# A decode block on one core: `w_out` in 96 partitions, the gated MLP in nine chunks of 96, and a query projection with one head to each group of 32 partitions

## The chip, the core and the metric

The kernel runs on one core of one Trainium2 chip. The metric is the device time of one execution in microseconds, the median of three runs. The core has a matrix engine (PE, with its weight loads listed as PEld), a vector engine (DVE), a scalar engine (ACT), GpSimd (POOL) and a sync engine (SP) that here does nothing but issue transfers. Transfers between HBM and the on-chip SBUF are carried by 16 DMA engines. Matmul results are written to PSUM.

## The reference, cut to what matters

Batch 4, one new token each, D = 640. Attention has 32 heads of 128 over a cache of 4096 positions; the gated MLP has 2 x 864 columns (F = 1728, Fh = 864). Everything is bf16 at the border.

```python
xn = _layernorm(x)
# attention: read the whole key and value cache
q = (xn @ wq).reshape(B, 1, 32, 128).transpose(0, 2, 1, 3)
p = softmax(einsum('bhqd,bhkd->bhqk', q, k_cache) * 128 ** -0.5)
A = (einsum('bhqk,bhkd->bhqd', p, v_cache)).transpose(...).reshape(B, 1, 4096) @ wo
# gated MLP
z = gelu(xn @ w_in)
z1, z2 = z[..., :864], layernorm(z[..., 864:])
g = w_sp * z2 + b_sp
Bm = (z1 * g) @ w_out
out = x + A + Bm
```

The two caches are 4 x 32 x 4096 x 128 bf16 each, 134 MB; the weights are small beside them (`wq` and `wo` 5.2 MB each, `w_in` 2.2 MB, `w_out` 1.1 MB).

## The kernel before, in words

**Tiles.** The cache is cut into 32 key tiles and 32 value tiles. Tile i holds four heads (head group i // 4) of one batch row (i % 4): 4 x 4096 positions, laid over 128 partitions, so that each head has 32 partitions and each partition 128 positions of 128 numbers, 32 KB that lie together in HBM. One tile is 4096 KB and one transfer.

**Slots and the order of transfers.** Five SBUF slots of tile size (`kv`, L69) rotate. The first three hold weights: `wq` in two pieces (L87 to L90) and `w_sb`, in which `w_in` and `w_out` lie side by side (L97 to L104). `w_out` has 864 rows of 1280 bytes. Before, its first 768 rows go to 128 partitions, six rows each (L101), and the other 96 rows to 96 partitions, one row each (L104). Then SP issues key tiles 0 and 1 and from there on, by the list of L125 to L132, a value tile and a key tile in turn. `pump()` (L137) issues the next one as soon as the program has passed the work on the tile that had the slot; on the chip the issue waits for that work through semaphores. `wo` comes in eight pieces of 640 KB (L147), the last one in four.

**Before the loop.** `xn` is normalised and transposed to `xnT` (128 partitions x 5 chunks x 32 columns, of which 4 are used). The query projection (L211 to L226) runs in two rounds r. In a round the four head groups g of that round each write 32 partitions of one PSUM tile: 5 chunks x 4 groups = 20 matmuls of 512 columns, and one DVE copy makes `q_rows[r]`. A row of `q_rows[r]` is then one head group and batch row, its 512 columns the four heads of that group.

**`stage_q(i)`** (L379) spreads the query of tile i over all partitions: a matmul with a repeated column of the identity as weights copies one row of `q_rows` to 128 partitions (512 columns, L384), and four ACT copies of 32 partitions each take the right head's 128 columns (L394).

**`gmlp()`** (L268) computes the gated MLP transposed: for each half t of `w_in` and each of seven chunks of its columns (six of 128, one of 96), five matmuls give `zT` (L276, 70 in all). DVE copies `zT` in two pieces (L283, L284) into `zz`, which POOL has cleared (L262), and computes the gelu with one ACT tanh. The sums of z2 and of its square are 14 matmuls of four columns with a column of ones (L302). After the layernorm and the gate, 14 matmuls with `w_out` add to `out_ps` (L366).

**The loop** over the 32 key tiles (L568) is in an order written by hand (`manual_schedule`, for PE, DVE, ACT and SP). For tile i in two halves: DVE multiplies the half with the query in place (`product`, L400), adds the two halves of the head dimension (`fold_half`, L409), PE adds up to eight numbers (`sums`, L418) and DVE the rest (`row_sums`, L429). `head_max` (L436) finds the maximum over each head's 32 partitions, negated, `exps` (L445) scales it on ACT to `nb` (L448) and makes the exponentials with their sums, a head at a time (L453). `weighted` (L462) multiplies them with the value tile on PE. `stage_q(i + 2)` stands in the middle of iteration i. Once in four tiles `group_den`, `group_pick`, `group_turn` and `group_proj` (L484 to L536) finish a head group and add its product with `wo` to `out_ps`.

**The end.** Value tile 31 comes in four pieces (L113), and its 128 matmuls (L625) have the value tile as weights. Then `o_n_last` (L633), eight matmuls with the last `wo` (L530), two copies and two transfers out (L640 to L643).

**Waits of SP.** Each transfer waits, besides for its slot, for the landing of the transfer eight before it in the program, whose semaphore it takes over (the first eight are free of that; three of the eight are small ones that ACT issues at L83, L94 and L95).

Of the kernel before, what the change touches and what calls it, by code (L numbers as in the profile page):

```python
# [9 lines left out]
FP32 = mybir.dt.float32  # L10
BF16 = mybir.dt.bfloat16
ACT = mybir.ActivationFunctionType
ALU = mybir.AluOpType
AX = mybir.AxisListType
# [7 lines left out]
def kernel(  # L22
# [14 lines left out]
    nc = tc.nc  # L37
    P = nc.NUM_PARTITIONS
    Bsz, Sq, D = A_x.shape
    _, H, S, Dh = A_k_cache.shape  # L40
    HD = A_wq.shape[1]
    F = B_w_in.shape[1]
    Fh = F // 2
    DC = D // P
    scale_qk = float(Dh) ** -0.5
# [3 lines left out]
    HT = 4  # L49
    HG = H // HT  # L50
    NT = HG * Bsz
    LN = P // HT
# [2 lines left out]
    HD2 = Dh // 2  # L55
    RW = 8
    SLOT = NC * Dh
    NFF = Fh // P
    NFC = NFF + 1
    FT = Fh - NFF * P  # L60
    NOH = D // 2
    QD = 32
    CB = 4
    NG = NC // CB
    GW = CB * Dh
    MC = CB * HT

    const = ctx.enter_context(tc.tile_pool(name="const", bufs=1))
    kv = ctx.enter_context(tc.tile_pool(name="kv", bufs=KV_SLOTS))  # L69
    wop = ctx.enter_context(tc.tile_pool(name="wop", bufs=WO_BUFS))  # L70
    work = ctx.enter_context(tc.tile_pool(name="work", bufs=1))
    small = ctx.enter_context(tc.tile_pool(name="small", bufs=2))
    PSUM = bass.MemoryType.PSUM
    ps_s = ctx.enter_context(tc.tile_pool(name="ps_s", bufs=2, space=PSUM))
    ps_pv = ctx.enter_context(tc.tile_pool(name="ps_pv", bufs=2, space=PSUM))
    ps_m = ctx.enter_context(tc.tile_pool(name="ps_m", bufs=3, space=PSUM))
# [9 lines left out]
    wq_parts = []  # L86
    for c0, c1 in ((0, HT), (HT, DC)):  # L87
        t = slot("wq")[:, 0 : (c1 - c0) * HD].rearrange("p (c n) -> p c n", n=HD)
# [9 lines left out]
    w_in_sb = w_sb[:, 0 : DC * F].rearrange("p (c n) -> p c n", c=DC)  # L98
    w_out_sb = w_sb[:, DC * F : DC * F + NFC * D].rearrange("p (k n) -> p k n", k=NFC)
    nc.sync.dma_start(out=w_in_sb, in_=B_w_in.rearrange("(p c) n -> p c n", c=DC))  # L100
    nc.sync.dma_start(  # L101
        out=w_out_sb[:, 0:NFF, :], in_=B_w_out[0 : NFF * P].rearrange("(p k) n -> p k n", k=NFF)
    )
    nc.sync.dma_start(out=w_out_sb[:FT, NFF, :], in_=B_w_out[NFF * P : Fh])  # L104

    def kv_view(cache, i):
        hg, b = divmod(i, Bsz)
# [51 lines left out]
    ident = const.tile([P, P], BF16)  # L159
# [2 lines left out]
    nc.vector.memset(ones_row[:], 1.0)  # L162
    eps_tile = const.tile([P, 1], FP32)
    nc.vector.memset(eps_tile[:], eps)
    ones_sq = const.tile([P, P], FP32)
    nc.vector.memset(ones_sq[:], 1.0)

    NACC = 2
    p_m = [const.tile([P, NG, QD], BF16, name=f"pm{b}") for b in range(Bsz)]
    acc = [const.tile([P, HT, QD], FP32, name=f"acc{g}") for g in range(NACC)]  # L170
# [9 lines left out]
    for i in range(NSTAT):  # L180
# [5 lines left out]
        out=rstd[:], in_=mv[:, 1:2], func=ACT.Sqrt, bias=eps_tile[:Bsz], scale=1.0  # L186
# [4 lines left out]
        out=xn_bf[:],  # L191
        in0=x_bf[:],
        scalar1=mv[:, 0:1],
        scalar2=rstd[:],
        op0=ALU.subtract,
# [5 lines left out]
    for c in range(DC):  # L201
        nc.tensor.transpose(
            out=xnT_ps[:, c, :], in_=xn_v[:, c, :], identity=ident[:Bsz, :Bsz]
# [5 lines left out]
    QB = HG // CB  # L209
    q_rows = []  # L210
    for r in range(QB):  # L211
        q_ps = ps_pv.tile([P, GW], FP32, tag="pv", name="q_ps")
        for c in range(DC):
            t, i = wq_parts[c]
            for g in range(CB):
                hg = r * CB + g
                nc.tensor.matmul(  # L217
                    out=q_ps[g * QD : (g + 1) * QD, :],
                    lhsT=xnT[:, c, :],
                    rhs=t[:, i, hg * GW : (hg + 1) * GW],  # L220
                    start=(c == 0),
                    stop=(c == DC - 1),
                )
        rows = const.tile([P, GW], BF16, name=f"q_rows{r}")
        nc.vector.tensor_copy(out=rows[:], in_=q_ps[:])  # L225
        q_rows.append(rows)  # L226

    pick = const.tile([P, 2, CB, HT, QD], FP32)
# [3 lines left out]
        out=hot[:],  # L232
        in_=ident[:].rearrange("p (g t m) -> p t m g", g=P // QD, t=2),
        axis=AX.X,
        op=ALU.add,
    )
    for a in range(2):
        for t in range(2):
            nc.vector.tensor_copy(
                out=pick[:, a, :, :, 2 * a + t],  # L240
# [16 lines left out]
        )  # L257

    gm = {}
    for name in ("zz", "gw", "gt", "gz"):  # L260
        gm[name] = work.tile([P, 2, NFC, Bsz], FP32, name=name)
    nc.gpsimd.memset(gm["zz"][:], 0.0)  # L262
    gm["sq"] = work.tile([P, NFC, Bsz], FP32, name="sq")
    gm["st"] = work.tile([1, 5 * Bsz], FP32, name="st")
    gm["ac"] = work.tile([1, 2 * Bsz], FP32, name="ac")
    gm["yT"] = work.tile([P, NFC, Bsz], BF16, name="yT")

    def gmlp():  # L268
        zz, gw, gt, gz, sq = (gm[n] for n in ("zz", "gw", "gt", "gz", "sq"))
        zT = ps_pv.tile([P, 2, NFC, Bsz], FP32, tag="pv", name="zT")  # L270
        for t in range(2):
            f1 = t * Fh + NFF * P
            w_t = w_in_sb[:, :, t * Fh : f1].rearrange("p c (f k) -> p c k f", k=NFF)
            for k in range(NFC):
                for c in range(DC):
                    nc.tensor.matmul(  # L276
                        out=zT[: P if k < NFF else FT, t, k, :],
                        lhsT=w_t[:, c, k, :] if k < NFF else w_in_sb[:, c, f1 : f1 + FT],
                        rhs=xnT[:, c, 0:Bsz],
                        start=(c == 0),  # L280
                        stop=(c == DC - 1),
                    )
        nc.vector.tensor_copy(out=zz[:, :, 0:NFF, :], in_=zT[:, :, 0:NFF, :])  # L283
        nc.vector.tensor_copy(out=zz[:FT, :, NFF, :], in_=zT[:FT, :, NFF, :])  # L284
        nc.vector.tensor_tensor(out=gw[:], in0=zz[:], in1=zz[:], op=ALU.mult)
        nc.vector.tensor_scalar(
            out=gw[:], in0=gw[:], scalar1=0.044715, scalar2=1.0, op0=ALU.mult, op1=ALU.add
# [5 lines left out]
        nc.vector.tensor_scalar(  # L293
            out=gt[:], in0=gt[:], scalar1=1.0, scalar2=0.5, op0=ALU.add, op1=ALU.mult
        )
        nc.vector.tensor_tensor(out=gz[:], in0=zz[:], in1=gt[:], op=ALU.mult)
        nc.vector.tensor_tensor(out=sq[:], in0=gz[:, 1, :, :], in1=gz[:, 1, :, :], op=ALU.mult)

        s_ps = ps_m.tile([1, 2 * Bsz], FP32, tag="m", name="ln_ps")
        for src, at in ((gz[:, 1, :, :], 0), (sq[:], Bsz)):  # L300
            for k in range(NFC):
                nc.tensor.matmul(  # L302
                    out=s_ps[:, at : at + Bsz],
                    lhsT=ones_sq[:, 0:1],
                    rhs=src[:, k, :],
                    start=(k == 0),
                    stop=(k == NFC - 1),
                )
        st, ac = gm["st"], gm["ac"]
        mean_t = st[:, 0:Bsz]  # L310
        ex2_t = st[:, Bsz : 2 * Bsz]
        var_t = st[:, 2 * Bsz : 3 * Bsz]
        rst_t = st[:, 3 * Bsz : 4 * Bsz]
        tmp_t = st[:, 4 * Bsz : 5 * Bsz]
        nc.vector.tensor_scalar(
            out=st[:, 0 : 2 * Bsz],
            in0=s_ps[:],
            scalar1=1.0 / float(Fh),
            scalar2=None,
            op0=ALU.mult,  # L320
# [27 lines left out]
        ac_sb = work.tile([P, 2 * Bsz], FP32, name="ac_sb")  # L348
        nc.scalar.copy(out=ac_sb[:], in_=ac_ps[:])
        nc.vector.tensor_tensor(  # L350
            out=sq[:],
            in0=gz[:, 1, :, :],
            in1=ac_sb[:, None, 0:Bsz].to_broadcast([P, NFC, Bsz]),
            op=ALU.mult,
        )
        nc.vector.tensor_tensor(
            out=sq[:],
            in0=sq[:],
            in1=ac_sb[:, None, Bsz : 2 * Bsz].to_broadcast([P, NFC, Bsz]),
            op=ALU.add,  # L360
        )
        nc.vector.tensor_tensor(out=gm["yT"][:], in0=gz[:, 0, :, :], in1=sq[:], op=ALU.mult)
        for k in range(NFC):
            w = P if k < NFF else FT
            for half in range(2):
                nc.tensor.matmul(  # L366
                    out=out_sum(half),
                    lhsT=gm["yT"][:w, k, :],
                    rhs=w_out_sb[:w, k, half * NOH : (half + 1) * NOH],
                    start=False,  # L370
                    stop=False,
                )
# [6 lines left out]
    def stage_q(i):  # L379
        hg, b = divmod(i, Bsz)  # L380
        r, g = divmod(hg, CB)
        row = g * QD + b
        qb_ps = ps_m.tile([P, HT, Dh], FP32, tag="m", name="qbc_ps")
        nc.tensor.matmul(  # L384
            out=qb_ps[:],
            lhsT=ident[:, row : row + 1].to_broadcast([P, P]),
            rhs=q_rows[r][:],
            start=True,
            stop=True,
        )  # L390
        qbcs[i] = small.tile([P, Dh], BF16, name="qbc", bufs=3)
        for hh in range(HT):
            ps = slice(hh * LN, (hh + 1) * LN)
            nc.scalar.copy(out=qbcs[i][ps, :], in_=qb_ps[ps, hh, :])  # L394

    def half_of(i, half):
        return k_tiles[i][:, half * HC : (half + 1) * HC, :]
# [46 lines left out]

    def exps(i):  # L445
        hg, b = divmod(i, Bsz)
        nb = small.tile([P, 1], FP32, name="nb")
        nc.scalar.mul(out=nb[:], in_=maxes.pop(i)[:], mul=scale_qk)  # L448
        s_sb, a = scores.pop(i), acc[hg % NACC]
        pm = p_m[b][:].rearrange("p g (t c h) -> p g t c h", t=2, c=CB)  # L450
        for hh in range(HT):
            ps = slice(hh * LN, (hh + 1) * LN)
            nc.scalar.activation(  # L453
                out=pm[ps, :, b % 2, :, hh],
                in_=s_sb[ps, :].rearrange("p (g c) -> p g c", c=CB),
                func=ACT.Exp,
                bias=nb[ps],
                scale=scale_qk,
                accum_out=a[ps, hh, b : b + 1],
            )  # L460

# [212 lines left out]
```

## Time and profile before

| What | Before |
|---|---|
| Median of 3 runs (lowest, highest) | 666.81 us (666.65, 666.91) |
| The profiled execution's own time | 666.78 us |
| Its span, first to last instruction | 665.0 us |
| Busy: PE, DVE, ACT, POOL | 309.9, 499.5, 127.1, 4.7 us |
| Read from HBM | 282.24 MB |
| Rate over the span | 424 GB/s |
| Mean granted PE clock | 0.715 of full |

The span leaves out 1.78 us that belong to the execution's time. An engine's busy time says how long it had work, not that it set the end: DVE is the busiest and is idle a quarter of the time. The DMA rows count packets; a packet is one contiguous piece of a transfer, and each of the 16 engines also writes one 4-byte completion per transfer. The trace keeps a start, a duration and a size for each packet.

### The profile page before, as it was taken

Reading aid. Unit: us, or ns where it says so; the run is one execution under the profiler, and the core shown is the slowest. Engines: PE = TensorE matmul, PEld = TensorE weight load, DVE = VectorE, ACT = ScalarE, POOL = GpSimd, SP = SyncE. Lnnn points to the kernel's source line nnn. Section 1 sums busy time; section 2 is a strip of 40 time slices with the busy share of each in tenths; the row PEclk is TensorE's granted clock in tenths of the full one; section 3 lists DMA queues with packets and bytes.
Section 4 is the critical chain, followed back from the end, with each engine's and each line's share of the span. In section 5 each row is a group of like instructions: output and inputs, shape, how many; then the busy total and the mean of one; then the engine's idle time right before and its main releaser. Section 6 shows DMA issues by size and latency. Waiting matters only on the chain.

```text
span 665.0 us, 5142 instructions
## 1 busy us (share of the span) xinstructions
PE 309.9 (47%) x2033; PEld 130.3 (20%) x2033; DVE 499.5 (75%) x350; ACT 127.1 (19%) x441; POOL 4.7 (1%) x15
## 2 busy tenths in 40 slices
PE   2536443445436235553238443355443655338466
PEld 1312111211112111321113111131111312113124
DVE  2299797877788777788777697777787899776970
ACT  0302222102222111222111222111222122111121
POOL 2000000000000000000000000000000000000000
PEclk9656766877767777776776856788765678776575
DMA  9999999999999999999999999999999999999996
GB/s 367 430 440 417 434 436 426 433 430 429 436 420 440 426 430 437 426 431 428 432 433 424 435 434 424 438 421 440 427 430 436 423 436 426 433 432 430 431 430 274
DMA packets 11972, 282.58 MB, mean 425 GB/s; under 512 B 1344, under 2 KB 1964, under 8 KB 3244
## 3 DMA queue, kind: packets, MB, share of 16 engines
q1 hardware_dynamic: 11928, 282.25, 99.2%
q8 instruction: 16, 0.26, 0.2%
q14 instruction: 8, 0.07, 0.0%
q10 hardware_dynamic: 20, 0.01, 0.0%
HBM read 282.24 MB, written 0.01 MB: 424 GB/s over the span
## 4 chain that ended last, share of the span: by engine, by line
DMA 68%; DVE 23%; PE 6%; issue 2%; SPq 0%; DVEq 0%
DMA k_nat<-in_A_k_cache_dram 62%; DVE k_nat L400 12%; DVE k_nat L409 7%; PE s_ps L418 4%; DMA v_nat<-in_A_v_cache_dram 4%; DVE s_sb L429 2%; DMA wq<-in_A_wq_dram 2%; PE pv L470 1%; PE q_ps L217 1%; DVE m L438 0%; DVE mt L440 0%; DVE o_n L513 0%; DVE nm L442 0%; PE out_ps L530 0%; SPq L120 0%
## 5 line engine op out<-in xcount | busy, mean ns | idle before, releaser
L400 DVE TENSOR_TENSOR k_nat<-k_nat,qbc 128x8192 bf16<-128x8192 bf16 x64 | 282.7, 4417 | 104.6 <-DMA k_nat<-in_A_k_cache_dram 104.3
L418 PE MATMUL s_ps<-k_nat,ident 128*128 128x512 bf16 x512 | 183.8, 523 | 327.0 <-DVE k_nat L409 327.0
L418 PEld LDWEIGHTS <-ident 128*128 128x128 bf16 x512 | 62.3, 122 | 430.7 <-issue 356.8
L409 DVE TENSOR_TENSOR k_nat<-k_nat 128x4096 bf16<-128x4096 bf16 x64 | 146.0, 2281 | 0.0
L448 ACT ACTIVATE nb<-nm 128x1 f32<-128x1 f32 x32 | 6.5, 203 | 355.1 <-DVE nm L442 355.1
L470 PE MATMUL pv<-v_nat,pm 128*32 128x512 bf16 x992 | 71.0, 438 | 3.7 <-DMA v_nat<-in_A_v_cache_dram 3.7
L453 ACT ACTIVATE pm<-s_sb,nb 32x128 bf16<-32x128 f32 x128 | 71.7, 560 | 2.7
L394 ACT CAST qbc<-qbc_ps 32x128 bf16<-32x128 f32 x128 | 32.8, 256 | 133.1 <-PE qbc_ps L384 132.0
L429 DVE TENSOR_REDUCE s_sb<-s_ps 128x64 f32<-128x512 f32 x64 | 43.6, 682 | 3.1 <-PE s_ps L418 3.1
L470 PEld LDWEIGHTS <-pm 128*32 128x32 bf16 x992 | 25.9, 109 | 55.3 <-issue 36.9
L453 ACT ACTIVATION_READ_ACCUMULATOR pm<-s_sb,nb 32x1 f32 x128 | 30.1, 235 | 0.0
L502 PEld LDWEIGHTS o_ps<-o_rows,pick 128*128 128x128 f32 x112 | 20.1, 269 | 2.1 <-issue 1.4
L502 PE MATMUL o_ps<-o_rows,pick 128*128 128x128 f32 x112 | 19.5, 347 | 0.0
L384 PE MATMUL qbc_ps<-q_rows,ident 128*128 128x512 bf16 x32 | 17.5, 552 | 0.0
L482 ACT COPY o_rows<-pv 128x512 f32<-128x512 f32 x16 | 9.4, 585 | 27.5 <-PE pv L470 27.5
L494 DVE RECIPROCAL rden<-den 128x1 f32<-128x1 f32 x7 | 1.2, 168 | 15.6 <-PE den L486 15.6
L438 DVE TENSOR_REDUCE m<-s_sb 128x1 f32<-128x128 f32 x32 | 9.2, 286 | 1.1
L225 DVE CAST q_rows<-q_ps 128x512 bf16<-128x512 f32 x2 | 1.4, 692 | 10.6 <-PE q_ps L217 10.6
L440 DVE STREAM_TRANSPOSE mt<-m 128x32 f32<-128x32 f32 x32 | 6.8, 212 | 1.1
L217 PE MATMUL q_ps<-wq,xnT 128*32 128x512 bf16 x40 | 4.1, 552 | 7.3 <-DMA wq<-in_A_wq_dram 7.3
L442 DVE TENSOR_REDUCE nm<-mt 128x1 f32<-128x32 f32 x32 | 6.0, 186 | 1.1
L384 PEld LDWEIGHTS <-ident 128*128 128x128 bf16 x32 | 4.4, 141 | 8.6 <-issue 8.6
(83 smaller groups left out, 73.4 us busy)
## 6 DMA issues: line engine op xcount, KB each, us to landing
k_nat<-in_A_k_cache_dram SPq DMA_DIRECT2D x32, 4096.0 KB, 41.2
v_nat<-in_A_v_cache_dram SPq DMA_DIRECT2D x31, 4096.0 KB, 35.7
wo<-in_A_wo_dram SPq DMA_DIRECT2D x7, 640.0 KB, 42.3
wq<-in_A_wq_dram SPq DMA_DIRECT2D x1, 4096.0 KB, 12.8
w_sb<-in_B_w_in_dram SPq DMA_DIRECT2D x1, 2160.0 KB, 19.5
v_nat<-in_A_v_cache_dram SPq DMA_DIRECT2D x1, 2048.0 KB
wq<-in_A_wq_dram SPq DMA_DIRECT2D x1, 1024.0 KB, 14.8
v_nat<-in_A_v_cache_dram SPq DMA_DIRECT2D x1, 1024.0 KB
```

The source lines that it names most:

```text
L217: nc.tensor.matmul(out=q_ps[g * QD : (g + 1) * QD, :], lhsT=xnT[:, c, :], rhs=t[:, i, hg * GW : (hg + 1) * GW], start=(c == 0), stop=(c == ...
L384: nc.tensor.matmul(out=qb_ps[:], lhsT=ident[:, row : row + 1].to_broadcast([P, P]), rhs=q_rows[r][:], start=True, stop=True,)
L394: nc.scalar.copy(out=qbcs[i][ps, :], in_=qb_ps[ps, hh, :])
L400: nc.vector.tensor_tensor(out=half_of(i, half), in0=half_of(i, half), in1=qbcs[i][:, None, :].to_broadcast([P, HC, Dh]), op=ALU.mult,)
L409: nc.vector.tensor_tensor(out=t[:, :, 0:HD2], in0=t[:, :, 0:HD2], in1=t[:, :, HD2:Dh], op=ALU.add)
L418: nc.tensor.matmul(out=s[:], lhsT=ident[:], rhs=t[:, :, g * RW : (g + 1) * RW], start=(g == 0), stop=(g == n - 1),)
L429: nc.vector.tensor_reduce(out=scores[i][:, half * HC : (half + 1) * HC], in_=sums_ps.pop((i, half))[:], axis=AX.X, op=ALU.add,)
L438: nc.vector.tensor_reduce(out=m1[:], in_=scores[i][:], axis=AX.X, op=ALU.max)
L453: nc.scalar.activation(out=pm[ps, :, b % 2, :, hh], in_=s_sb[ps, :].rearrange("p (g c) -> p g c", c=CB), func=ACT.Exp, bias=nb[ps], scale= ...
L470: nc.tensor.matmul(out=pvs[hg, a][cg * QD : (cg + 1) * QD, :], lhsT=pm[:, g, :], rhs=v_nat[:, g * CB : (g + 1) * CB, :], start=(t == 0 and ...
L482: nc.scalar.copy(out=o[:].rearrange("p c d -> p (c d)"), in_=pvs.pop((hg, a))[:])
L502: nc.tensor.matmul(out=o_ps[:], lhsT=pick[:, a, c, :, :].rearrange("p h q -> p (h q)"), rhs=o[:, c, :], start=(a == 0 and c == 0), stop=(a ...
```

## The change

`w_out` is loaded in one transfer of 96 partitions with nine rows each, and the MLP's 864 columns are cut into nine chunks of 96 throughout, so that no chunk is short. The two sums of the layernorm become one matmul of 72 columns and a DVE reduction. The query projection puts head hh of every head group in partitions 32 hh to 32 hh + 31, so that a row of a group is spread by one matmul of 128 columns, with weights `of_row` made once on POOL, and one ACT copy of 128 partitions. The factor 128 ** -0.5 moves from the exponentials into the copy of `q_ps`, and the ACT multiplication `nb` is gone.

```diff
-    NFF = Fh // P
-    NFC = NFF + 1
-    FT = Fh - NFF * P
+    NFC = 9
+    FL = Fh // NFC
...
-    nc.sync.dma_start(
-        out=w_out_sb[:, 0:NFF, :], in_=B_w_out[0 : NFF * P].rearrange("(p k) n -> p k n", k=NFF)
-    )
-    nc.sync.dma_start(out=w_out_sb[:FT, NFF, :], in_=B_w_out[NFF * P : Fh])
+    nc.sync.dma_start(out=w_out_sb[:FL], in_=B_w_out.rearrange("(p k) n -> p k n", k=NFC))
...
+    of_row = const.tile([P, Bsz, HT, LN], BF16)
+    nc.gpsimd.tensor_copy(
+        out=of_row[:],
+        in_=ident[:].rearrange("p (h q) -> p q h", q=LN)[:, 0:Bsz, :, None].to_broadcast(
+            [P, Bsz, HT, LN]
+        ),
+    )
...
-            t, i = wq_parts[c]
-            for g in range(CB):
-                hg = r * CB + g
+            t, at_c = wq_parts[c]
+            by_head = t[:, at_c, :].rearrange("p (g h d) -> p h g d", h=HT, d=Dh)
+            for hh in range(HT):
                 nc.tensor.matmul(
-                    out=q_ps[g * QD : (g + 1) * QD, :],
+                    out=q_ps[hh * LN : (hh + 1) * LN],
                     lhsT=xnT[:, c, :],
-                    rhs=t[:, i, hg * GW : (hg + 1) * GW],
+                    rhs=by_head[:, hh, r * CB : (r + 1) * CB, :],
...
-        nc.vector.tensor_copy(out=rows[:], in_=q_ps[:])
+        nc.vector.tensor_scalar(
+            out=rows[:], in0=q_ps[:], scalar1=scale_qk, scalar2=None, op0=ALU.mult
+        )
...
-    nc.gpsimd.memset(gm["zz"][:], 0.0)
...
-            f1 = t * Fh + NFF * P
-            w_t = w_in_sb[:, :, t * Fh : f1].rearrange("p c (f k) -> p c k f", k=NFF)
+            w_t = w_in_sb[:, :, t * Fh : (t + 1) * Fh].rearrange("p c (f k) -> p c k f", k=NFC)
             for k in range(NFC):
                 for c in range(DC):
                     nc.tensor.matmul(
-                        out=zT[: P if k < NFF else FT, t, k, :],
-                        lhsT=w_t[:, c, k, :] if k < NFF else w_in_sb[:, c, f1 : f1 + FT],
+                        out=zT[:, t, k, :],
+                        lhsT=w_t[:, c, k, :],
...
-        nc.vector.tensor_copy(out=zz[:, :, 0:NFF, :], in_=zT[:, :, 0:NFF, :])
-        nc.vector.tensor_copy(out=zz[:FT, :, NFF, :], in_=zT[:FT, :, NFF, :])
+        nc.vector.tensor_copy(out=zz[:], in_=zT[:])
...
-        for src, at in ((gz[:, 1, :, :], 0), (sq[:], Bsz)):
-            for k in range(NFC):
-                nc.tensor.matmul(
-                    out=s_ps[:, at : at + Bsz],
-                    lhsT=ones_sq[:, 0:1],
-                    rhs=src[:, k, :],
-                    start=(k == 0),
-                    stop=(k == NFC - 1),
-                )
+        nc.tensor.matmul(
+            out=s_ps[:], lhsT=ones_sq[:FL, 0:1], rhs=gz[:, 1:3], start=True, stop=True
+        )
...
+        nc.vector.tensor_reduce(
+            out=st[:, 0 : 2 * Bsz].rearrange("o (s b) -> o s b", s=2),
+            in_=s_ps[:].rearrange("o s k b -> o s b k"),
+            axis=AX.X,
+            op=ALU.add,
+        )
...
-        row = g * QD + b
-        qb_ps = ps_m.tile([P, HT, Dh], FP32, tag="m", name="qbc_ps")
+        qb_ps = ps_m.tile([P, Dh], FP32, tag="m", name="qbc_ps")
         nc.tensor.matmul(
             out=qb_ps[:],
-            lhsT=ident[:, row : row + 1].to_broadcast([P, P]),
-            rhs=q_rows[r][:],
+            lhsT=of_row[:, b, :, :].rearrange("p h q -> p (h q)"),
+            rhs=q_rows[r][:, g, :],
...
-        for hh in range(HT):
-            ps = slice(hh * LN, (hh + 1) * LN)
-            nc.scalar.copy(out=qbcs[i][ps, :], in_=qb_ps[ps, hh, :])
+        nc.scalar.copy(out=qbcs[i][:], in_=qb_ps[:])
...
-        nb = small.tile([P, 1], FP32, name="nb")
-        nc.scalar.mul(out=nb[:], in_=maxes.pop(i)[:], mul=scale_qk)
-        s_sb, a = scores.pop(i), acc[hg % NACC]
+        s_sb, a, nm = scores.pop(i), acc[hg % NACC], maxes.pop(i)
...
-                bias=nb[ps],
-                scale=scale_qk,
+                bias=nm[ps],
+                scale=1.0,
```

The MLP's further DVE steps are the same instructions on 96 partitions and 72 (or 36) columns in place of 128 partitions and 56 (or 28), and its product with `w_out` has 18 matmuls in place of 14. By the order of the instructions, the changed kernel issues the same transfers as before on SP, in the same order, with the one of 96 rows of 11,520 bytes in place of the two; on ACT 32 copies stand in place of 128, and the 32 `nb` are gone; nothing in the loop changes its place.

More of the change, by code (lines that the diff above doesn't have):

```diff
@@ L57 @@
     SLOT = NC * Dh
-    NFF = Fh // P
-    NFC = NFF + 1
-    FT = Fh - NFF * P
+    NFC = 9
+    FL = Fh // NFC
+    assert FL * NFC == Fh and FL <= P
     NOH = D // 2
@@ L211 @@
     for r in range(QB):
-        q_ps = ps_pv.tile([P, GW], FP32, tag="pv", name="q_ps")
+        q_ps = ps_pv.tile([P, CB, Dh], FP32, tag="pv", name="q_ps")
         for c in range(DC):
-            t, i = wq_parts[c]
-            for g in range(CB):
-                hg = r * CB + g
+            t, at_c = wq_parts[c]
+            by_head = t[:, at_c, :].rearrange("p (g h d) -> p h g d", h=HT, d=Dh)
+            for hh in range(HT):
                 nc.tensor.matmul(
-                    out=q_ps[g * QD : (g + 1) * QD, :],
+                    out=q_ps[hh * LN : (hh + 1) * LN],
                     lhsT=xnT[:, c, :],
-                    rhs=t[:, i, hg * GW : (hg + 1) * GW],
+                    rhs=by_head[:, hh, r * CB : (r + 1) * CB, :],
                     start=(c == 0),
@@ L223 @@
                 )
-        rows = const.tile([P, GW], BF16, name=f"q_rows{r}")
-        nc.vector.tensor_copy(out=rows[:], in_=q_ps[:])
+        rows = const.tile([P, CB, Dh], BF16, name=f"q_rows{r}")
+        nc.vector.tensor_scalar(
+            out=rows[:], in0=q_ps[:], scalar1=scale_qk, scalar2=None, op0=ALU.mult
+        )
         q_rows.append(rows)
@@ L259 @@
     gm = {}
-    for name in ("zz", "gw", "gt", "gz"):
-        gm[name] = work.tile([P, 2, NFC, Bsz], FP32, name=name)
-    nc.gpsimd.memset(gm["zz"][:], 0.0)
-    gm["sq"] = work.tile([P, NFC, Bsz], FP32, name="sq")
+    for name in ("zz", "gw", "gt"):
+        gm[name] = work.tile([FL, 2, NFC, Bsz], FP32, name=name)
+    gm["gz"] = work.tile([FL, 3, NFC, Bsz], FP32, name="gz")
     gm["st"] = work.tile([1, 5 * Bsz], FP32, name="st")
     gm["ac"] = work.tile([1, 2 * Bsz], FP32, name="ac")
-    gm["yT"] = work.tile([P, NFC, Bsz], BF16, name="yT")
+    gm["yT"] = work.tile([FL, NFC, Bsz], BF16, name="yT")
     def gmlp():
-        zz, gw, gt, gz, sq = (gm[n] for n in ("zz", "gw", "gt", "gz", "sq"))
-        zT = ps_pv.tile([P, 2, NFC, Bsz], FP32, tag="pv", name="zT")
+        zz, gw, gt, gz = (gm[n] for n in ("zz", "gw", "gt", "gz"))
+        zT = ps_pv.tile([FL, 2, NFC, Bsz], FP32, tag="pv", name="zT")
         for t in range(2):
-            f1 = t * Fh + NFF * P
-            w_t = w_in_sb[:, :, t * Fh : f1].rearrange("p c (f k) -> p c k f", k=NFF)
+            w_t = w_in_sb[:, :, t * Fh : (t + 1) * Fh].rearrange("p c (f k) -> p c k f", k=NFC)
             for k in range(NFC):
@@ L295, in gmlp @@
         )
-        nc.vector.tensor_tensor(out=gz[:], in0=zz[:], in1=gt[:], op=ALU.mult)
-        nc.vector.tensor_tensor(out=sq[:], in0=gz[:, 1, :, :], in1=gz[:, 1, :, :], op=ALU.mult)
-        s_ps = ps_m.tile([1, 2 * Bsz], FP32, tag="m", name="ln_ps")
-        for src, at in ((gz[:, 1, :, :], 0), (sq[:], Bsz)):
-            for k in range(NFC):
-                nc.tensor.matmul(
-                    out=s_ps[:, at : at + Bsz],
-                    lhsT=ones_sq[:, 0:1],
-                    rhs=src[:, k, :],
-                    start=(k == 0),
-                    stop=(k == NFC - 1),
-                )
+        nc.vector.tensor_tensor(out=gz[:, 0:2], in0=zz[:], in1=gt[:], op=ALU.mult)
+        sq = gz[:, 2, :, :]
+        nc.vector.tensor_tensor(out=sq, in0=gz[:, 1, :, :], in1=gz[:, 1, :, :], op=ALU.mult)
+        s_ps = ps_m.tile([1, 2, NFC, Bsz], FP32, tag="m", name="ln_ps")
+        nc.tensor.matmul(
+            out=s_ps[:], lhsT=ones_sq[:FL, 0:1], rhs=gz[:, 1:3], start=True, stop=True
+        )
         st, ac = gm["st"], gm["ac"]
@@ L314, in gmlp @@
         tmp_t = st[:, 4 * Bsz : 5 * Bsz]
+        nc.vector.tensor_reduce(
[4 more added lines that the diff above has]
+        )
         nc.vector.tensor_scalar(
             out=st[:, 0 : 2 * Bsz],
-            in0=s_ps[:],
+            in0=st[:, 0 : 2 * Bsz],
             scalar1=1.0 / float(Fh),
@@ L350, in gmlp @@
         nc.vector.tensor_tensor(
-            out=sq[:],
+            out=sq,
             in0=gz[:, 1, :, :],
-            in1=ac_sb[:, None, 0:Bsz].to_broadcast([P, NFC, Bsz]),
+            in1=ac_sb[:FL, None, 0:Bsz].to_broadcast([FL, NFC, Bsz]),
             op=ALU.mult,
@@ L356, in gmlp @@
         nc.vector.tensor_tensor(
-            out=sq[:],
-            in0=sq[:],
-            in1=ac_sb[:, None, Bsz : 2 * Bsz].to_broadcast([P, NFC, Bsz]),
+            out=sq,
+            in0=sq,
+            in1=ac_sb[:FL, None, Bsz : 2 * Bsz].to_broadcast([FL, NFC, Bsz]),
             op=ALU.add,
         )
-        nc.vector.tensor_tensor(out=gm["yT"][:], in0=gz[:, 0, :, :], in1=sq[:], op=ALU.mult)
+        nc.vector.tensor_tensor(out=gm["yT"][:], in0=gz[:, 0, :, :], in1=sq, op=ALU.mult)
         for k in range(NFC):
-            w = P if k < NFF else FT
             for half in range(2):
@@ L367, in gmlp @@
                     out=out_sum(half),
-                    lhsT=gm["yT"][:w, k, :],
-                    rhs=w_out_sb[:w, k, half * NOH : (half + 1) * NOH],
+                    lhsT=gm["yT"][:, k, :],
+                    rhs=w_out_sb[:FL, k, half * NOH : (half + 1) * NOH],
                     start=False,
```

## The prediction, as it was put on record

> **What bounds the kernel.** I read the shares by slice first, then the DMA queues and issues, then stretches of the span, and last the chain of waits near the end.
>
> ```profile
> DMA  9999999999999999999999999999999999999996
> ...
> q1 hardware_dynamic: 11928, 282.25, 99.2%
> q8 instruction: 16, 0.26, 0.2%
> q14 instruction: 8, 0.07, 0.0%
> ```
>
> The 16 DMA engines are 90% busy or more in 39 of 40 slices, and queue q1, which carries every tile, fills 99.2% of 16 engines' span. Two queues that fetch instructions use the same engines; they matter below.
>
> ```profile
> 64.00:640.00 576.00, 265.93 (x1566) 107.22 (x1568) 456.39 (x290) 110.41 (x396) 0.00 (x0) 0.72 1.00 431
> 640.00:660.00 20.00, 15.61 (x228) 9.56 (x218) 4.18 (x7) 3.62 (x11) 0.00 (x0) 0.67 0.94 392
> 660.00:665.00 5.00, 1.91 (x24) 0.98 (x24) 0.66 (x2) 0.41 (x1) 0.00 (x0) 0.50 0.15 52
> ```
>
> The columns are the stretch, its length, the busy time of PE, PEld, DVE, ACT and POOL, the PE clock, the DMA share and GB/s. From 64 to 640 us the DMA share is 1.00 at 431 GB/s. No engine holds a transfer up there, although the chain of waits gives DVE 23% of the span.
>
> ```profile
> k_nat<-in_A_k_cache_dram SPq DMA_DIRECT2D x32, 4096.0 KB, 41.2
> v_nat<-in_A_v_cache_dram SPq DMA_DIRECT2D x31, 4096.0 KB, 35.7
> ```
>
> A tile takes 9.7 us at 431 GB/s (4.19 MB), but its median is 41.2 or 35.7 us from issue to landing, so 31 or 26 us of that are queueing. Whatever delays an issue by less than about 26 us, or speeds it up, leaves the landings where they are. This cover carries most of what follows. It ends only where the last value tile lands:
>
> ```profile
> 632.46 27.63 DMA v_nat<-in_A_v_cache_dram
> 660.09 0.05 issue
> 660.14 0.60 PE o_last L625 x16
> 660.75 0.02 issue
> 660.77 0.19 DVE o_n_last L633
> 660.96 0.04 issue
> 661.00 1.36 PE out_ps L530 x8
> 662.36 0.02 issue
> 662.38 0.48 DVE res L641
> ```
>
> So the time is the DMA engines' work up to 660.09 us, then 2.8 us of instructions, the transfer out up to 665.0, and 1.78 us outside the span: 666.78. The change touches none of the instructions after 660.09.
>
> **The change, part by part.**
>
> *`w_out`.* The bytes stay. What can change is the time on each DMA engine. By the packet records an engine's part of the 768-row transfer is 8 packets of 7680 B, 2.30 us from one completion write to the next, and of the 96-row one 6 packets of 1280 B, 0.32 us: together 2.62 us. After it are 6 packets of 11,520 B. Packets of 7680 B follow each other every 0.287 us, those of `w_in` (17,280 B) every 0.641; a straight line between gives 0.428, so 2.57 us with a completion write. **Gain 0.05 us.** Below, the gain can't exceed the whole second transfer, 0.32. The bound above comes from an uneven use of the engines or of their paths into SBUF. Were only 12 engines used (eight packets each, 3.42 us), the loss would be 0.8 us. The nearest row speaks against it: the old 96-row transfer gave all 16 engines six packets, mean 0.0573 us each, and the 512 packets of the same size in the last `wo`, over 128 partitions, took 0.0575. I take the row.
>
> [...]
>
> *SP.* One issue fewer (0.53 us at 3.09 us). The second key tile takes over a semaphore of an earlier transfer now and need not wait until 13.5 us for `wq` (9.4 us). Both move issues behind 8 MB that are already queued: nothing.
>
> *Gated MLP.* Its end frees the slot of `w_sb`, and value tile 1 is issued at 33.21 us. The matmuls for `zT`: 70 in 3.75 us, so 90 in 4.82, +1.07. The sums: 28 passes in 0.85 us become one matmul of 72 f32 columns, about 0.35 (a 128-column one is 0.347, a 4-column one 0.166), and a reduction, 0.22 (0.186 for 32 columns, 0.286 for 128): -0.28. Second copy of `zT` gone: -0.13. Eight DVE steps with 16 columns more, about 0.02 each: +0.17. The product with `w_out`: 14 in 2.03 us, so 18 in 2.61, +0.58. Together **+1.4 us**, issue at 34.6. Queued ahead are key tile 0, which landed at 34.8, key tile 1, value tile 0 and key tile 2, until 34.8 + 3 x 9.7 = 64 us. Even ten times that delay stays behind it. DVE could not start key tile 0 before 34.79 anyway.
>
> *Query projection.* Again 40 matmuls of 512 columns (4.1 us); their input is four runs of 128 now, which no row here shows. Between no cost and twice the time, +4.1 us, all of it lies before 34.79. The scaled copy stands where a 0.69 us copy stood. `of_row` is one POOL operation (a memset of twice its size is 0.95 us), ready long before 17.6 us.
>
> *In the loop.* Per tile the spreading matmul has 128 columns in place of 512 (0.552 us; between the 0.168 of a 4-column and the 0.347 of a 128-column f32 one), ACT does one copy (between 0.256 for 32 partitions and 0.585 for 128x512) in place of four, and `nb` (0.203) is gone. Over 32 tiles that takes some 8 us off PE and 24 + 6.5 us off ACT. All lies under the DMA: ACT is 19% busy, and of the 104.6 us that DVE waited at L400, 104.3 were for key tiles to land. Exponentials come 0.3 us sooner, and so do value slots, ahead of 26 us of queue. **Nothing**, between -0.1 and +0.1. If the cover were gone, the query would come about 1 us sooner in each of 32 tiles.
>
> *The end.* After the last key tile: row sums, maximum, exponentials, done at 649.7, while value tile 30 lands at 650.16. PE then works until 659.5 and waits 0.67 us. Gone is only `nb`, off the path: nothing.
>
> **Sum:** 666.78 - 0.05 = 666.7 us, 0.1 below the median of 666.81. A measurement of this kernel can tell about 0.2% from no change, 1.3 us.
>
> **What is left over** is which DMA engine ends last. Completion writes of one transfer spread over 1.06 us at the first, and over 3.5 us in the second half. The steps are instruction fetches: 16 of 16 KB, 1.07 us each, and 8 of 8 KB. Each pushes one engine's tiles back, by about 1.55 us and 0.7 us. Most of the big ones go round: the same few engines are hit about 300 us apart. Eight or so engines with two hits each end last, within 0.5 us of each other. The changed kernel has 47 more PE instructions of some 3740 and about 130 fewer on ACT. So fetches move by microseconds, and one of the small ones may go; either is worth up to 0.4 us, which is my forecast's own spread: 666.3 to 667.1.
>
> [...]
>
> **The rivals.**
>
> 1. *A third fetch on a late engine* (slower). If the longer PE program crosses one more block boundary, or the round shifts, a block lands on an engine that already has two, before its last value packets. Price 1.55 us: 666.8 + 1.55 = 668.4, +0.23%. It decides only before about 660 us and on one of the late half. For it: 47 more instructions, and that fetches do repeat on engines. [...] 7%.
> 2. *The late part of that, or lanes.* A fetch near 659 us catches an engine in its last pieces, up to 1.0 us, or 96 partitions cost 0.8 after all: 667.6. 6%.
> 3. *The last matmuls at full clock.* PE has clock 0.50 from 649 us on. Eight matmuls of L530 took 0.71 us at 140.4, where the clock was 1.00, and 1.36 at the end: -0.65. If the 16 of L625 shrink likewise, by up to half of 0.60, that gives -0.9: 665.9. For it: PE's activity changes, and the clock switched some 75 times. Against it: the matmuls from 650 on stay as they are. 8%.
> 4. *Both lucky:* that clock, and about 0.6 us fewer fetches on the late engines: 665.3, -0.23%. 4%.
> 5. *The change doesn't do what it says*, say one transfer that is split badly. The instruction order shows one copy of 96 x 5760, and 96 rows went evenly before; the price is that of case 2, in whose chance it is.
>
> **How the numbers follow.** Forecast 75%, rivals 7, 6, 8, 4. Within 0.2% are the forecast, 2 and 3, which is 89%; I keep 2% of it for what I haven't seen and give 87. Slower: rival 1 and half of that, 8%. Faster: rival 4 and the other half, 5%. The range reaches from rival 3 to rival 2 with 0.1 around: 665.8 to 667.7.
>
> **What would show it.** Right: q1 with 11,784 packets (11,928 less 224 packets of `w_out` and 16 completion writes, and 96 more), the same 282.25 MB, still 431 GB/s from 64 to 640 us; ACT busy near 97 us and PE near 300; value tile 1 issued near 34.6 us and the last value piece landing near 660.1. Wrong: a DMA share clearly under 1.00 between 64 and 640 us; that landing more than 1 us off; or a wait of DVE at L400 for the query in place of a key tile.

## The result, and the profile after

The changed kernel takes **668.79 us** (median of 7 runs, 668.52 to 669.23), the kernel before 666.81 (7 runs, 666.65 to 666.91): a ratio of 1.0031, 95% interval 1.002 to 1.0042. It is **2.0 us slower**, outside the predicted range of 665.8 to 667.7. The profiled execution took 668.76 us, its span is 667.0, so 1.76 us lie outside the span, as before.

The rows by slice and by queue in the page of the changed kernel, read as in the prediction:

```profile
DMA  9999999999999999999999999999999999999996
GB/s 371 382 424 434 435 427 426 432 430 431 432 430 431 428 432 429 427 432 436 427 425 437 424 434 434 432 425 432 427 432 432 424 434 432 427 433 428 427 431 273
...
q1 hardware_dynamic: 11784, 282.25, 99.1%
q8 instruction: 16, 0.26, 0.2%
q14 instruction: 7, 0.06, 0.0%
```

The DMA engines are as "busy" as before in every slice, and the bytes are the same. But the second slice, from 16.7 to 33.4 us, moves only 382 GB/s. In the page of the kernel before that slice has 430:

```profile
GB/s 367 430 440 417 434 436 426 433 430 429 436 420 440 426 430 437 426 431 428 432 433 424 435 434 424 438 421 440 427 430 436 423 436 426 433 432 430 431 430 274
```

48 GB/s less over 16.7 us is 0.8 MB not moved, which at 431 GB/s is 1.9 us, about the whole difference. The busy share doesn't show it, 9 tenths in both: an engine whose packet takes longer is busy all the longer. The later stretches, with the columns of the prediction:

```profile
64.00:640.00 576.00, 266.05 (x1594) 108.53 (x1594) 462.91 (x293) 86.28 (x292) 0.00 (x0) 0.73 1.00 430
640.00:660.00 20.00, 15.09 (x207) 8.08 (x206) 6.05 (x8) 3.42 (x10) 0.00 (x0) 0.76 0.98 411
660.00:665.00 5.00, 3.01 (x60) 1.91 (x57) 0.66 (x2) 0.41 (x1) 0.00 (x0) 0.50 0.38 138
```

Up to 640 us the rate is the old one (430 beside 431 by the rows; by the packet records both kernels move 247.9 MB in that stretch), and what was not moved early is moved late: 411 GB/s where the kernel before had 392, then 138 in place of 52. The chain of waits ends in the same way, only later:

```profile
633.98 28.04 DMA v_nat<-in_A_v_cache_dram
662.02 0.04 issue
662.06 0.60 PE o_last L623 x16
...
664.30 0.48 DVE res L639
```

The last value piece landed at 660.09 us before and lands at 662.02 now, 1.93 later. What follows it takes as long as it did, to within 0.1 us.

**Where in the second slice.** Four microseconds of each kernel, first the one before, then the changed one, with the columns of the stretches above (the last number is GB/s):

```profile
21.00:25.00 4.00, 3.75 (x70) 3.66 (x70) 0.00 (x0) 0.48 (x1) 0.00 (x0) 0.50 1.08 423
```

```profile
21.00:25.00 4.00, 2.97 (x18) 2.97 (x18) 0.00 (x0) 0.00 (x0) 0.00 (x0) 0.52 1.10 293
```

The packet records say whose packets these are. The 96 packets of `w_out` took 0.736 us each on the mean (median 0.763), not the 0.43 that the prediction drew from packets of other sizes. Only the first six ran at 0.43. Six to an engine make **4.41 us** where the prediction had 2.57. The packets are slow from 20.1 us on, 2 us before the MLP's first matmul, and the rate is back at 426 GB/s from 26.0 us on, while the MLP's matmuls go on to 37 us. The first 16 packets of key tile 0, right behind, are slow as well: they took 1.62 us on the mean, those after them 1.22.

### The profile page after: what moved, and what is told of

It reads as the page before. It is cut to its first block, busy times and chain, and to the rows that moved or that the text cites. A ratio compares the mean times of both kernels' runs of the same rounds, so it can differ in the third digit from the quotient of the medians.

```text
span 667.0 us, 5046 instructions
## 1 busy us (share of the span) xinstructions
PE 316.0 (47%) x2031; PEld 140.5 (21%) x2031; DVE 499.2 (75%) x350; ACT 96.3 (14%) x313; POOL 5.2 (1%) x15
## 3 DMA queue, kind: packets, MB, share of 16 engines
q1 hardware_dynamic: 11784, 282.25, 99.1%
## 4 chain that ended last, share of the span: by engine, by line
DMA 62%; DVE 27%; PE 8%; issue 2%; SPq 0%; ACT 0%; DVEq 0%
DMA k_nat<-in_A_k_cache_dram 54%; DVE k_nat L400 14%; DVE k_nat L409 9%; PE s_ps L418 4%; DMA v_nat<-in_A_v_cache_dram 4%; DMA w_sb<-in_B_w_in_dram 3%; PE zT L280 2%; DVE s_sb L429 2%; PE pv L468 1%; DVE m L438 1%; DVE mt L440 0%; DVE nm L442 0%; DVE o_n L511 0%; PE out_ps L528 0%; SPq L117 0%
## 5 line engine op out<-in xcount | busy, mean ns | idle before, releaser
L418 PE MATMUL s_ps<-k_nat,ident 128*128 128x512 bf16 x512 | 187.1, 531 | 320.3 <-DVE k_nat L409 320.3
L418 PEld LDWEIGHTS <-ident 128*128 128x128 bf16 x512 | 63.0, 123 | 425.9 <-issue 362.1
L451 ACT ACTIVATE pm<-s_sb,nm 32x128 bf16<-32x128 f32 x128 | 71.7, 560 | 357.4 <-DVE nm L442 355.7
L429 DVE TENSOR_REDUCE s_sb<-s_ps 128x64 f32<-128x512 f32 x64 | 43.7, 682 | 2.7 <-PE s_ps L418 2.7
L451 ACT ACTIVATION_READ_ACCUMULATOR pm<-s_sb,nm 32x1 f32 x128 | 30.1, 235 | 0.0
L394 ACT CAST qbc<-qbc_ps 128x128 bf16<-128x128 f32 x32 | 8.4, 266 | 129.3 <-PE qbc_ps L386 129.3
L500 PEld LDWEIGHTS o_ps<-o_rows,pick 128*128 128x128 f32 x112 | 18.7, 252 | 2.0 <-issue 1.3
L280 PE MATMUL zT<-xnT,w_sb 128*96 128x4 bf16 x90 | 15.6, 312 | 3.7 <-DMA w_sb<-in_B_w_in_dram 3.7
L280 PEld LDWEIGHTS <-w_sb 128*96 128x96 bf16 x90 | 15.6, 267 | 3.9 <-DMA w_sb<-in_B_w_in_dram 3.9
L229 DVE TENSOR_SCALAR q_rows<-q_ps 128x512 bf16<-128x512 f32 x2 | 1.4, 691 | 10.6 <-PE q_ps L221 10.6
L386 PE MATMUL qbc_ps<-q_rows,of_row 128*128 128x128 bf16 x32 | 9.1, 290 | 0.0
```

Source lines behind the costliest of these rows:

```text
L280: nc.tensor.matmul(out=zT[:, t, k, :], lhsT=w_t[:, c, k, :], rhs=xnT[:, c, 0:Bsz], start=(c == 0), stop=(c == DC - 1),)
L386: nc.tensor.matmul(out=qb_ps[:], lhsT=of_row[:, b, :, :].rearrange("p h q -> p (h q)"), rhs=q_rows[r][:, g, :], start=True, stop=True,)
L394: nc.scalar.copy(out=qbcs[i][:], in_=qb_ps[:])
L418: nc.tensor.matmul(out=s[:], lhsT=ident[:], rhs=t[:, :, g * RW : (g + 1) * RW], start=(g == 0), stop=(g == n - 1),)
L429: nc.vector.tensor_reduce(out=scores[i][:, half * HC : (half + 1) * HC], in_=sums_ps.pop((i, half))[:], axis=AX.X, op=ALU.add,)
L451: nc.scalar.activation(out=pm[ps, :, b % 2, :, hh], in_=s_sb[ps, :].rearrange("p (g c) -> p g c", c=CB), func=ACT.Exp, bias=nm[ps], scale=1.0,
```

## The experiments

The loss is in one transfer, so the theories are about that transfer. **S**, on the author's assumption that each of the 16 DMA engines serves neighbouring partitions, which no trace here shows: the engines would now read from places 69,120 B apart in HBM (61,440 before), and this spacing is bad. **L**: 96 partitions in place of 128 are what slows it. **P**: the size of the packets. The rival to all three is that the query part costs the time. For `w_out`, the time of the packets on an engine (their sum over 16) is given beside the medians:

| Kernel | `w_out` goes as | us on an engine | Median, us | Ratio to before, 95% |
|---|---|---|---|---|
| before | 128 x 7680 B, 96 x 1280 B | 2.34 + 0.34 | 666.81 | |
| changed | 96 x 11,520 B | 4.41 | 668.79 | 1.0031 (1.002 to 1.0042) |
| e1_query_part | as before | 2.35 + 0.35 | 666.89 | 1.0 (0.9991 to 1.0009) |
| e2_eight_and_one | 96 x 10,240 B, 96 x 1280 B | 3.81 + 0.51 | 668.66 | 1.0027 (1.0016 to 1.0038) |
| e3_128_partitions | 128 x 8640 B | 2.61 | 666.54 | 0.9995 (0.9985 to 1.0004) |
| e4_row_packets | 96 x 9 x 1280 B | 5.02 | 669.25 | 1.0036 (1.0023 to 1.0049) |
| e5_spread | 64 x 11,520 B, 32 x 11,520 B | 3.17 | 667.65 | 1.0012 (1.0003 to 1.0021) |
| e6_stacked | 64 x 11,520 B, 32 x 11,520 B | 4.78 | 669.21 | 1.0035 (1.0022 to 1.0049) |
| e7_overlap | 128 x 7680 B, 128 x 1280 B | 2.33 + 0.44 | 666.59 | 0.9997 (0.9988 to 1.0005) |
| e9_both | as e7 | | 666.63 | 0.9997 (0.9988 to 1.0006) |

The kernel before, run beside them, had medians of 666.97 (e1 to e4) and 666.80 (e5 to e9). Median less the time on an engine is between 663.8 and 664.5 us in all nine kernels that have both: that one term carries most of the differences. With the first 16 packets of key tile 0 added, one to an engine (their means go from 1.21 us in e3, e7 and e9 over 1.48 before and 1.62 in the changed kernel to 1.85 in e5), what remains is between 662.5 and 662.8 us in all ten, so that these two terms leave hardly anything to explain.

**e1_query_part**: the kernel before with the query part of the change alone (`of_row`, a head to each group of partitions, one copy, no `nb`).

```diff
+                    out=q_ps[hh * LN : (hh + 1) * LN],
+                    rhs=by_head[:, hh, r * CB : (r + 1) * CB, :],
...
+        nc.scalar.copy(out=qbcs[i][:], in_=qb_ps[:])
```

> The kernel before with the query part of the change alone; w_out and the gated MLP stay as they were. All three theories put the 2.0 us into the w_out transfer, whose packets of 11,520 B took 0.736 us each in the changed kernel where 0.43 was expected, so that 16 engines lost about 1.9 us each. They expect no change here: 666.8 us, within 0.3. The rival that the loss comes from the query part (its strided matmul input, later key work) expects 668.8.

Measured 666.89 us, ratio 1.0. The query part neither costs nor gains anything, and its rival falls.

**e2_eight_and_one**: the changed kernel, 96 partitions kept, spacing in HBM (by the assumption of S, 61,440 B) as before. The MLP's columns follow; that part of the edit is left out here.

```diff
-    nc.sync.dma_start(out=w_out_sb[:FL], in_=B_w_out.rearrange("(p k) n -> p k n", k=NFC))
+    nc.sync.dma_start(
+        out=w_out_sb[:FL, 0 : NFC - 1, :],
+        in_=B_w_out[0:M8].rearrange("(p k) n -> p k n", k=NFC - 1),
+    )
+    nc.sync.dma_start(out=w_out_sb[:FL, NFC - 1, :], in_=B_w_out[M8:Fh])
```

> The changed kernel, still with 96 partitions and nine chunks of 96, but w_out in two transfers: 96 rows of 10,240 B (eight of w_out's rows each), then 96 of 1280 B. [...] Theory S (the spacing of the 16 streams in HBM is what slows them): packets at about 0.38 us, the two transfers 2.6 us together, 666.8 us. Theory L (96 partitions in place of 128, six neighbouring ones to a DMA engine, is what slows them): packets at about 0.65 us, 4.4 us, 668.7 us. Theory P (long packets to 96 partitions by their size): slow too, 668.5.

Measured 668.66 us, packets of 10,240 B at 0.635 us. S falls, as far as its assumption holds; L gave 0.65 and 668.7.

**e3_128_partitions**: the other way round, 128 partitions and the changed kernel's spacing (by the assumption of S, 69,120 B).

```diff
+    nc.sync.dma_start(
+        out=w_sb[:, DC * F : DC * F + PW],
+        in_=B_w_out.rearrange("k n -> (k n)").rearrange("(p x) -> p x", p=P),
+    )
...
-                    rhs=w_out_sb[:FL, k, half * NOH : (half + 1) * NOH],
+                    rhs=w_out_sb[:FL, k % 6, half * NOH : (half + 1) * NOH],
```

> The changed kernel, but the same 1.1 MB of w_out go to 128 partitions as 8640 B each, without regard to rows, and the MLP's last product reads chunks 0 to 5 for its nine, so its weights are not the right ones; all instructions but the transfer stay. [...] Theory S: packets stay slow, about 0.55 us in place of 0.33, 668.8 us. Theory L: packets at 0.33 us, 2.6 us for the transfer, 666.8 us. Theory P: fast or half way, since 8640 B is nearer to the 7680 that were fast.

Measured 666.54 us, every packet at 0.326 us. The same four microseconds of this kernel:

```profile
21.00:25.00 4.00, 3.60 (x21) 3.60 (x22) 0.00 (x0) 0.00 (x0) 0.00 (x0) 1.00 1.15 491
```

(Shares above 1.00 stand in such short stretches of every kernel, so that only the comparison counts.) Beside it stand the 293 of the changed kernel, with the same bytes and all other instructions alike. Only the shape of the transfer differs: 128 partitions and 8640 B in place of 96 and 11,520 B. That also clears the rest of the changed MLP and its matmuls.

**e4_row_packets**: 96 partitions in one transfer, but chunk k holds rows 96 k to 96 k + 95, so that each packet is one row of 1280 B, 54 to an engine. By the assumption of S the engines would start 7680 B apart.

```diff
-B_w_out.rearrange("(p k) n -> p k n", k=NFC)
+B_w_out.rearrange("(k p) n -> p k n", k=NFC)
...
-.rearrange("p c (f k) -> p c k f", k=NFC)
+.rearrange("p c (k f) -> p c k f", k=NFC)
```

> [...] Theory S: no slowdown, 54 packets at 0.052 us are 2.8 us, 0.2 more than before, 667.0 us. Theory L: as slow as the changed kernel or more, 4.4 us, 668.7 us. Theory P: fast, since 96 packets of 1280 B ran at full pace in the kernel before.

Measured 669.25 us: P falls too. Its packets show what the prediction had missed. The first 96 of the 864 took 0.055 us, those behind mostly 0.08 to 0.12. A transfer of 96 such packets, the row on which the prediction leaned, is nearly over before the slowdown sets in: in the kernel before 86 of the 96 took 0.055, and ten of the last 18 up to 0.088.

**Which partitions.** L doesn't say why. Theory **B** is that it matters which partitions a transfer writes. Its numbers rest on an assumption of the author's: packets to partitions 32 to 95 run at the full 0.43 us, those to 0 to 31 alone, to 64 to 95 alone or to 0 to 63 take twice that, 0.85. The prediction and the expectation of e9 speak of paths or ways into SBUF; no trace shows these, only the pace by partitions. The next two kernels cut the changed kernel's transfer into the same two sizes, with different partitions. From the 0.43 us and four and two packets to an engine, B's estimate is 1.7 + 1.7 = 3.4 us for e5 and 3.4 + 1.7 = 5.1 us, less what the engines that are ahead give back, for e6. With the 664.1 us (before) to 664.4 us (changed) that the medians have beside `w_out`, that is 667.7 and 669.3.

```diff
+    w_out_rows = B_w_out.rearrange("(p k) n -> p k n", k=NFC)
+    for p0, p1 in ((32, FL), (0, 32)):
+        nc.sync.dma_start(out=w_out_sb[p0:p1], in_=w_out_rows[p0:p1])
```

> The changed kernel with its w_out transfer cut in two by partitions: 64 rows of 11,520 B to partitions 32 to 95 first, then 32 rows to partitions 0 to 31. [...] Theory C: any transfer to fewer than 128 partitions runs at about 240 GB/s, whichever they are: packets of 0.75 us in both parts, 4.4 us, 668.8 us. Theory D: only numbers of partitions that are no power of two are slow: both parts at 0.43, 2.6 us, 666.8 us. [...]

Measured 667.65 us, theory B's 667.7. Partitions 32 to 95 got their 64 packets at 0.432 us each, the pace of 128 partitions (26.7 B a ns; in e3 8640 B in 0.326 us, 26.5). The packets of partitions 0 to 31 rose to 0.88, where 0.85 was worked out; the first 16 of the 32 were still on their way up, from 0.43 to 0.78, so that the whole took 3.17 us, not 3.4. Part of the loss falls on key tile 0 behind them, whose first 16 packets took 1.85 us in place of 1.22.

e6_stacked has `((0, 64), (64, FL))` in the loop's header:

> As e5_spread, but cut at 64: 64 rows to partitions 0 to 63, then 32 rows to partitions 64 to 95. [...] Theory C: 4.4 us, 668.8. Theory D: 2.6 us, 666.8.

Measured 669.21 us, B's 669.3. Packets of partitions 0 to 63 settled at 0.82 to 0.92 us. Those of partitions 64 to 95, behind them, took 0.57 to 0.85, and the two parts together 4.78 us, where B had 5.1, less a part that it did not put in numbers. The two kernels in the four microseconds, e5_spread first:

```profile
21.00:25.00 4.00, 3.82 (x23) 3.83 (x23) 0.00 (x0) 0.00 (x0) 0.00 (x0) 0.58 1.17 365
```

```profile
21.00:25.00 4.00, 2.65 (x16) 2.65 (x16) 0.00 (x0) 0.00 (x0) 0.00 (x0) 0.53 1.19 286
```

Equal bytes, equal numbers of transfers and of packets, 365 against 286 GB/s: neither C (all below 128 are slow alike) nor D (powers of two are fast) can give that. Nor can S or P: packets and spacing are the same in both kernels, whichever engine serves which partition. B stands: served first, partitions 32 to 95 took 0.432 us a packet and partitions 0 to 63 0.82 to 0.92. Why the partitions differ so, no run shows.

**e7_overlap**: if 96 partitions are slow, the old kernel's second transfer must have cost something as well.

```diff
-    nc.sync.dma_start(out=w_out_sb[:FT, NFF, :], in_=B_w_out[NFF * P : Fh])
+    nc.sync.dma_start(out=w_out_sb[:, NFF, :], in_=B_w_out[Fh - P : Fh])
+    DUP = P - FT
...
-        nc.vector.tensor_copy(out=zz[:FT, :, NFF, :], in_=zT[:FT, :, NFF, :])
+        for p0, p1 in ((DUP, 2 * DUP), (2 * DUP, P)):
+            nc.vector.tensor_copy(out=zz[p0:p1, :, NFF, :], in_=zT[p0:p1, :, NFF, :])
```

> The kernel before, with its second w_out transfer widened from 96 to 128 partitions: the last 128 rows of w_out in place of the last 96, so that 32 rows are read twice and the MLP leaves the copies out. 41 KB more to read, 0.1 us. Theories B and C: the old 96-row transfer already cost something, which shows as packets of key tile 0 that are late by 0.3 to 0.6 us on nine engines; that goes, 0.3 us faster net, 666.6 us beside 666.9. Theory D the same. The reading of the prediction, that this transfer lost nothing: 0.1 us slower.

By the packet records of the kernel before (each packet's bytes spread evenly over its time), the rate falls to 342 to 386 GB/s in the 2 us in which its 96-row transfer ends and key tile 0 begins to arrive. In e7_overlap it is 404 in one half microsecond and 427 or more in the next ones. The first 16 packets of key tile 0 took 1.48 us on the mean before and 1.21 in e7_overlap: 0.27 us less on an engine, for 0.1 more in `w_out`. The median is 0.2 us lower, as that gives, but the interval, 0.9988 to 1.0005, takes in no change, and the 0.1 us slower of the prediction's reading too. So the slow packets are shown, and their price in the kernel's time isn't.

> The same kernel as e7_overlap once more, one look, to see whether the rate dip behind w_out stays away in a second profile: 430 GB/s throughout.

This one execution took 666.65 us. The dip of the old transfer stays away there too: after 404 in one half microsecond, 427 to 435 GB/s for 3 us. Then the rate is 419 to 425 for some 2.5 us, from about the time on at which a 16 KB instruction fetch runs, at 26.3 us; e3 has the same at its fetch, at 29.8.

**e9_both**: e7_overlap with the query part of e1.

> The kernel before with the two edits that the runs leave standing: the query part of the change, which by itself made no difference, and the last w_out transfer over 128 partitions, whose rate dip of some 0.3 us goes. Theory B, that only the ways into SBUF that a transfer can use count, and that all work of the engines lies under the transfers: 666.5 us, 0.2 to 0.4 below the kernel before, about 430 GB/s throughout behind w_out. The rival that shorter work on ACT and PE pays by itself expects clearly less, 666 us or below.

Measured 666.63 us, interval 0.9988 to 1.0006: with the intervals as they are, no version here is shown to beat the kernel before. The rival that less work on ACT and PE pays (666 or below) falls.

## Why the prediction was wrong, step by step

*`w_out`: the step that failed*, and the only one that cost time. The forecast was a gain of 0.05 us, with 2.57 us on an engine; it measured 4.41, a loss of 1.7 beside the 2.34 + 0.34 before. The first packets of key tile 0 behind it add 0.14 (1.62 us on the mean beside 1.48). Together that is nearly the 1.93 us by which the last value piece lands later. Two choices led there. The nearest row was taken for the price because the number of partitions and the packets to an engine matched, and its mean of 0.0573 us stood beside 0.0575 over 128 partitions. But that transfer has 123 KB, a ninth of the new one, and e4 shows that the first packets run at full pace. The mean hid the slow ones at its end, and most of its slowdown fell on the packets behind it, of key tile 0, which the prediction did not look at. And the bound of 0.8 us above was too small: it was worked out from 12 busy engines, 3.42 us, which no run shows. What the runs show is a pace that depends on the partitions: e5, which serves partitions 32 to 95 first, comes to 3.17 us on an engine, e6 to 4.78, and the changed kernel's one transfer took 4.41, 1.0 us more than that bound. An uneven use of the paths into SBUF was named as a source of loss, and then set aside by the one row.

*Rival 2* had the loss in this transfer ("96 partitions cost 0.8 after all"), at less than half of the price and with part of 6%. *Rival 1* forecast 668.4 by another mechanism, a third instruction fetch; q8 has 16 blocks as before, and the loss is complete before the first of them, at 29.6 us. That the number came close is chance. The 47 more PE instructions that spoke for it don't show either: the profile, which leaves control instructions out, has 2031 matmuls and as many weight loads, two fewer of each than before.

*The cover held*, and under more load than forecast. The MLP was to free its slot at 34.6 us; the SP row of the changed kernel has

```profile
46.44 0.33 SPq L117 DMA_DIRECT2D v_nat<-in_A_v_cache_dram  x1
```

so 13.2 us later than before, not 1.4. Its 90 matmuls took 15.64 us, 174 ns a pair, where 70 had taken 3.75, 54 ns a pair:

```profile
L280 PEld LDWEIGHTS <-w_sb x90: 247/268/268, 22.0 to 37.3; 128*96 128x96 bf16 x90
```

Before:

```profile
L276 PEld LDWEIGHTS <-w_sb x70: 125/144/198, 21.2 to 24.7; 128*128 128x128 bf16 x60, 128*96 128x96 bf16 x10
```

The columns after the count are the shortest, median and longest load in ns. DVE began key tile 0 at 43.7 in place of 34.8 us. e3 has the same late MLP (its issue is at 45.82 us) and takes 666.54 us: 13 us behind 26 us of queue cost nothing. So the step was mis-sized tenfold, and the reason given for its price of nothing was right.

*Query part and loop:* no time, as forecast. ACT 127.1 to 96.3 us busy (97 forecast). The parts that were forecast from the loop came (8.4 us off PE, 24.4 and 6.5 off ACT). But PE went up to 316.0 and not down to 300, mainly by the 11.9 us that those matmuls grew. *SP and the end:* as forecast; 11,784 packets in q1, one small instruction fetch fewer (8 to 7), the last landing to the end of the span as long as before. The clock of the last matmuls stayed at 0.50, so rivals 3 and 4 did not come. Of the signs, the landing of the last value piece more than 1 us off is the one that said "wrong"; a DMA share under 1.00 didn't, since slow packets keep an engine busy.

*Chances.* 87% for a change within 0.2% came from treating the partition question as settled by one short row. No other term of the sum had a bound as far from its value that would not lie behind the queue, so the doubt belonged there.

## What to carry to other kernels

In a kernel that the DMA engines bound, ask of each transfer not only how many bytes and packets it has and how many engines share it, but which partitions it writes: the same bytes in the same packets differed by 1.6 us on an engine (3.17 and 4.78) through that alone. Price a transfer from a row of like size in bytes, since a short one can end before its limit shows (in e4 the first 96 packets ran at 0.055 us, those behind mostly at 0.08 to 0.12), and look for its cost in the packets behind it (1.62 us in place of 1.22 in the changed kernel). A merge of transfers that leaves the full set of partitions isn't a saving in itself: here it cost 2.0 us.

## What the runs showed of the hardware

- In a transfer to partitions 0 to 95, packets to partitions 32 to 95 were slow too. In the changed kernel 84 of the 96 packets of `w_out` took 0.66 us or more, so at least 52 of the 64 to these partitions, which took 0.432 in e5. Nor is the 3.17 us reached that the same rows took there: it was 4.41. Why those packets wait is open; it wasn't tried.
- Weight loads of 96 columns took longer than loads of 128, and longer still where the columns lie apart. The means are 267 ns with a column every 18 B (changed), 264 with one every 16 B (e2), 194 side by side (e4; 192 in the short chunks of the kernel before), beside 144 for 128 columns, one every 12 B (before). The granted clock isn't it: in e3 it is 1.00 from 21 to 29 us and the load takes 267, and in the changed kernel it is 0.50 from 25 to 37 us for the same 267. Why the number of columns and their distance cost this, no run here tells.
